# A fixed instruction order, a new order within a slot, more buffers and a two-step weight decode in a top-k attention kernel followed by a gated feed-forward layer

## The chip, the cores and the metric

The kernel runs on one core of a Trainium2 chip. The metric is the device time of one execution in microseconds; the median of the runs is reported. A profile is one execution recorded by the hardware profiler.

The core has five engines with a queue of instructions each: TensorE (PE, matrix products), VectorE (DVE), ScalarE (ACT), GpSimd (POOL) and SyncE (SP), which here only issues DMAs. They work side by side and meet at semaphores.

## The reference

Attention over 8 batches, 8 heads, 576 positions and 64 features keeps, for each query, the 32 largest scores. Its output, laid out as 4608 tokens of 512 features, goes through a layer of width 2048 with the gate h*cos(h).

```python
scores = scale * np.matmul(q, k.transpose(0, 1, 3, 2))
kth = np.partition(scores, -top_k, axis=-1)[..., -top_k:-top_k + 1]
scores = np.where(scores >= kth, scores, -1000000000.0)
attn = np.exp(scores - np.max(scores, axis=-1, keepdims=True))
attn = attn / (np.sum(attn, axis=-1, keepdims=True) + 1e-09)
attn_out = np.matmul(attn, v)
x = attn_out.transpose(0, 2, 1, 3).reshape(B * S, H * D)
h = x @ w_in
g = h * np.cos(h)
return g @ w_out
```

q, k and v are float32. The two weight matrices arrive as 64-bit floats, which the chip reads as pairs of 32-bit words, so the kernel turns them into float32 itself ("decode").

## The kernel before

**Units and slots.** The attention is cut into 144 units: 128 tokens times one pair of heads (four pairs a token tile). The main loop runs 146 slots. In slot i three units are at work: `u` = unit i is in its top-k search, `w` = unit i−1 in its softmax, `x` = unit i−2 is transposed and multiplied by v. The scores of unit i+2 are computed at the end of the slot.

**One unit.** `scores` (L184) writes 128x1152 scores to PSUM, one buffer, and ACT copies them to the tile `s` (L192). `topk_round` runs four times: two MAX8 (L206) find eight maxima each for the two heads, and two MATCH_REPLACE8 (L209, not in the fourth round) strike them out; all on DVE. `bounds` (POOL, L216 and L221) makes the mask's and the exponent's bias from the maxima. `softmax` runs two Prelu activations (L228), which push what is under the bound far down, and two exponentials with their sums (L233), on ACT. `add_eps` (POOL, L240), `reciprocal` (DVE, L246) and `normalise` (POOL, L251) finish it, the last in the next slot. `transpose_main` (L264, PE; copies to `pT`, L265, ACT), `transpose_tail` (L272, L273) and `values` (L289; copy to `xT`, L294) make the output. The tiles of the transposes and of the values share two PSUM buffers.

**The feed-forward layer in pieces.** Tokens form blocks: two of 128, sixteen of 256, two of 128. `ff1` makes one piece of the first product (L334): eight matmul instructions at 256 columns. Two pieces fill a PSUM tile, which ACT scales into half of a chunk `g` (L344); four pieces fill the chunk of 128x1024. A chunk is then reduced to a quarter-period argument `x` by four POOL instructions (L359 to L362), goes through the sine on ACT (`sines`, L372) and is multiplied back on POOL (`gates`, L379). There are 72 chunks. `ff2` makes a piece of the second product: two accumulation steps, four matmul instructions of 512 columns (L391); eight pieces make a token tile, scaled by ACT (L397) and stored by SP (L399). Both products have 288 pieces, 576 in all. After the last unit's search (`ff["end"]`) the reduction and the gate run on DVE instead (L350, L353, L379).

**The feeder.** `feed(n)` places up to n pieces on PE. Each slot adds 4.2 to a credit that is capped at 6, and a piece costs 1. It prefers `ff2` of the oldest block if the chunks it needs are gated and all weights are decoded. Otherwise it takes `ff1`, if the block's attention is complete, its weights are decoded and fewer than `CHUNKS` = 5 chunks are held; a block gives its chunks back only when its last `ff2` piece is placed. What is left after the 146 slots is placed by the last loop, two pieces an iteration.

**Weights.** There are 32 weight chunks of 512 KB. `load_weights` issues the DMA from SP into a buffer of tag `x`, of which there are `XB` = 3, shared with the sine arguments. `decode_weights` runs three ACT (L114, L115, L118), three DVE (L119, L120, L124) and two POOL instructions (L127, L128). Four chunks are decoded in each of the first slots.

**What sets the order.** The code runs inside a tile framework. Without further notice the framework reorders the instructions by its own planner: the order in which the functions are called gives a priority, and the planner decides when each instruction takes its place in its engine's queue. Once placed, the queue of an engine is worked off as placed.

Of the kernel before, what the change touches and what calls it, by code (L numbers as in the profile page):

```python
# [16 lines left out]
P = 128  # L17
# [13 lines left out]
def kernel(  # L31
# [7 lines left out]
    out: bass.AP,  # L39
):  # L40
    nc = tc.nc
    B, H, D, S = qT.shape
    DM, DF = moe_w_in.shape
    NT = S // P
# [43 lines left out]
        w_out.append(w)  # L88
        chunks.append((moe_w_out[f * P : (f + 1) * P, :], w))
    staged = {}  # L90
    CHUNKS, XB = 5, 3

    def load_weights(i):
        if i >= len(chunks):
            return
        src, dst = chunks[i]
        if not DECODE:
            nc.sync.dma_start(out=dst, in_=src)
            return
        st = ffw.tile([P, CW, 2], I32, tag="x", name="st", bufs=XB)  # L100
        nc.sync.dma_start(out=st.rearrange("p w i -> p (w i)"), in_=src)
        staged[i] = st

    def decode_weights(i):
        if not DECODE:
            return
        st = staged.pop(i)
        lo, hi = st[:, :, 0], st[:, :, 1]
        w = chunks[i][1]
        wi = w.bitcast(I32)  # L110

        both = ffw.tile([P, 2, CW], F32, tag="g", name="lo_sg", bufs=CHUNKS)
        r, sg = both[:, 0].bitcast(I32), both[:, 1]
        nc.scalar.mul(out=r, in_=lo.bitcast(U32), mul=2.0**-29)  # L114
        nc.scalar.sign(sg, hi)  # L115


        nc.scalar.activation(out=w, in_=hi.bitcast(F32), func=AF.Abs)  # L118
        nc.vector.tensor_scalar(out=w, in0=w, scalar1=2.0**-15, scalar2=None, op0=ALU.max)  # L119
        nc.vector.tensor_scalar(  # L120
            out=wi, in0=wi, scalar1=896 << 20, scalar2=3,
            op0=ALU.bitwise_xor, op1=ALU.logical_shift_left,
        )
        nc.vector.tensor_scalar(  # L124
            out=wi, in0=wi, scalar1=0x7FFFFFFF, scalar2=None, op0=ALU.bitwise_and
        )
        nc.gpsimd.tensor_tensor(out=wi, in0=wi, in1=r, op=ALU.add)  # L127
        nc.gpsimd.tensor_tensor(out=w, in0=w, in1=sg, op=ALU.mult)  # L128
# [46 lines left out]
            )  # L175

    def scores(u):
        sc = ps.tile([P, 2, 2, 512], F32, tag="sc", name="sc", bufs=1)
        for h in range(2):
            for j in range(2):  # L180
                d = slice(j * D, (j + 1) * D)
                for b, q0, rows, r0 in u["parts"]:
                    st = pairs[b, u["hp"]]
                    nc.tensor.matmul(  # L184
                        sc[r0 : r0 + rows, j, h, 0:HS],
                        st["q"][d, q0 : q0 + rows],
                        st["k"][d, h * HS : (h + 1) * HS],
                        start=True,
                        stop=True,
                    )  # L190
        s = u["s"] = work.tile([P, 2, S], F32, tag="s", name="s", bufs=5)
        nc.scalar.copy(  # L192
            out=s.rearrange("p j (h w) -> p (j h) w", h=2),
            in_=sc.rearrange("p j h w -> p (j h) w")[:, :, 0:HS],
        )

    def topk_round(u, rnd):
# [23 lines left out]
        nc.gpsimd.tensor_tensor(out=nd, in0=nb[:, :, 0], in1=nb[:, :, 1], op=ALU.subtract)  # L221
        u["nb"], u["nd"] = nb, nd

    def softmax(u):

        s, nb, nd = u["s"], u.pop("nb"), u.pop("nd")
        for j in range(2):
            nc.scalar.activation(  # L228
                out=s[:, j], in_=s[:, j], func=AF.Prelu, bias=nb[:, j, 1:2], scale=SCALE, alpha=FAR
            )  # L230
        den = u["den"] = small.tile([P, 2], F32, tag="den", name="den")
        for j in range(2):
            nc.scalar.activation(  # L233
                out=s[:, j], in_=s[:, j], func=AF.Exp, bias=nd[:, j : j + 1], scale=1.0,
                accum_out=den[:, j : j + 1],
            )
# [65 lines left out]
    for w in widths:  # L302
# [6 lines left out]
        t0 += w  # L309


    ff = {"live": 0, "now": 0, "weights": 0, "credit": 0.0, "end": False}
    first = deque((blk, i) for blk in blocks for i in range(2 * NF * blk["w"] // 512))
    second = deque(
        (blk, i, f) for blk in blocks for i in range(blk["w"] // P) for f in range(0, NF, 2)
    )
    waiting = deque()
    sined = deque()

    def ff1(blk, i):  # L320
        w = blk["w"]
        nf = 256 // w
        part = i % 4
        if part == 0:
            blk["g"].append(ffw.tile([P, 1024], F32, tag="g", name="g", bufs=CHUNKS))
            ff["live"] += 1
        if part % 2 == 0:
            blk["mm"] = ps.tile([P, 512], F32, tag="mm", name="mm")
        g, mm = blk["g"][-1], blk["mm"]
        for a in range(nf):  # L330
            f = i * nf + a
            at = (part % 2 * nf + a) * w
            for c in range(NC):
                nc.tensor.matmul(  # L334
                    mm[:, at : at + w],
                    w_in[f // FC][:, c, (f % FC) * P : (f % FC + 1) * P],
                    blk["xT"][:, c],
                    start=c == 0,
                    stop=c == NC - 1,
                )  # L340
        if part % 2 == 0:
            return
        half = part // 2
        nc.scalar.mul(out=g[:, half * 512 : half * 512 + 512], in_=mm, mul=INV_2PI)  # L344
        if half == 0:
            return
        x = ffw.tile([P, 1024], F32, tag="x", name="x", bufs=XB)
        if ff["end"]:

            nc.vector.tensor_scalar(  # L350
                out=x, in0=g, scalar1=0.25, scalar2=MAGIC, op0=ALU.add, op1=ALU.add
            )
            nc.vector.scalar_tensor_tensor(  # L353
                out=x, in0=x, scalar=MAGIC, in1=g, op0=ALU.subtract, op1=ALU.subtract
            )
            waiting.append((blk, g, x, ff["now"], -TWO_PI_BELOW))
            return
        gp = nc.gpsimd
        gp.tensor_scalar(out=x, in0=g, scalar1=1.0, scalar2=0.25, op0=ALU.mult, op1=ALU.add)  # L359
        gp.tensor_scalar(out=x, in0=x, scalar1=1.0, scalar2=MAGIC, op0=ALU.mult, op1=ALU.add)  # L360
        gp.tensor_scalar(out=x, in0=x, scalar1=-MAGIC, scalar2=1.0, op0=ALU.add, op1=ALU.mult)  # L361
        gp.tensor_tensor(out=x, in0=g, in1=x, op=ALU.subtract)  # L362
        waiting.append((blk, g, x, ff["now"], TWO_PI_BELOW))

    def sines(least):

        ready = [c for c in waiting if c[3] < ff["now"]]
        if not ready or (len(ready) < least and ready[0][3] + 4 > ff["now"]):
            return
        for blk, g, x, _, scale in ready:  # L370
            waiting.popleft()
            nc.scalar.activation(out=x, in_=x, func=AF.Sin, bias=halfpi, scale=scale)  # L372
            sined.append((blk, g, x))

    def gates():
        while sined:
            blk, g, x = sined.popleft()
            eng = nc.vector if ff["end"] else nc.gpsimd
            eng.tensor_tensor(out=g, in0=g, in1=x, op=ALU.mult)  # L379
            blk["gated"] += 1  # L380
# [40 lines left out]
            ff1(blk, i)  # L421
            n, ff["credit"] = n - 1, ff["credit"] - 1

    def decode(k):
        for _ in range(k):
            i = ff["weights"]
            if i < len(chunks):
                decode_weights(i)
                load_weights(i + 2)
                ff["weights"] += 1  # L430

# [11 lines left out]

    load_qk(0, 0)
    load_weights(0)
    load_qk(0, 1)
    load_weights(1)
    scores(units[0])  # L450
    for hp in range(2, NP):
        load_qk(0, hp)
    for hp in range(NP):
        load_v(0, hp)
    scores(units[1])
    for i in range(NU + 2):
        ff["end"] = i >= NU
        u = units[i] if i < NU else None
        w = units[i - 1] if 0 < i <= NU else None
        x = units[i - 2] if i > 1 else None  # L460
        for f, b, hp in at_slot.get(i, []):
            f(b, hp)
        ff["credit"] = min(ff["credit"] + 4.2, 6.0)
        ff["now"] += 1
        if w:
            bounds(w)
        if x:
            normalise(x)
        if u:
            topk_round(u, 0)  # L470
        decode(1)
        if w:
            softmax(w)
        gates()
        feed(2)
        if x:
            transpose_main(x)
        if u:
            topk_round(u, 1)
        decode(1)  # L480
        feed(1)
        if x:
            transpose_tail(x)
        feed(6)
        if w:
            add_eps(w)
        sines(2)
        if u:
            topk_round(u, 2)
        decode(1)  # L490
        if x:
            values(x)
        if i + 2 < NU:
            scores(units[i + 2])
        if u:
            topk_round(u, 3)
        if w:
            reciprocal(w)
        decode(1)
    while first or second:  # L500
        ff["now"] += 1
        ff["credit"] = 2.0
        gates()
        sines(1)
        feed(2)
        if ff["credit"] == 2.0:
            ff["now"] += 4


# [35 lines left out]
```

## Time and profile before

| | us |
|---|---|
| median of three runs (1831.09 to 1840.1) | 1837.81 |
| the profiled execution's own time | 1836.45 |
| its span, first to last instruction | 1834.7 |

Busy times by stage, in us:

| stretch of the span | PE | DVE | ACT | POOL | granted PE clock |
|---|---|---|---|---|---|
| 0 to 245.5 | 162.93 | 230.30 | 166.37 | 152.59 | 0.88 |
| 245.5 to 1645 | 1311.13 | 1238.33 | 969.83 | 698.14 | 0.98 |
| 1645 to 1834.7 | 167.66 | 34.76 | 37.31 | 3.45 | 0.98 |

In the first stretch the weights are decoded beside the first units, and few feed-forward pieces exist yet. In the second the units run one slot after the other with pieces between. In the third only feed-forward pieces are left, but for the last two units. The busy time of PE contains the filling of its pipeline at each start of a run of matmuls, so it overstates how much of it is used.

A timeline row gives the start, the duration, the engine, the line, the operation with its tiles, how often it follows itself (xcount), and in brackets how long the engine had been idle before and what released it. A row of the waits names who waited for whom, the total in us, how often, and the longest.

### The profile page before, as it was taken

What the parts mean: (1) busy time and instruction counts of PE and PEld (TensorE: products, weight loads), DVE (VectorE), ACT (ScalarE), POOL (GpSimd) and SP (SyncE); (2) the same over time, 40 slices, a digit from 0 to 9 for tenths busy, and PEclk for the clock granted to TensorE, in tenths of its full rate; (3) what the DMA queues carried; (4) which work ended last, traced back from release to release, by engine and by line L of the source; (5) the groups of instructions that cost most, each with busy time, mean ns of one, the idle gap of its engine ahead of it and who ended that gap; (6) DMA issues with size and microseconds to landing.
All of it is one profiled execution on the core that took longest, in us unless ns stands there. A gap on an engine that the chain in (4) does not pass through costs nothing.

```text
span 1834.7 us, 26443 instructions
## 1 busy us (share of the span) xinstructions
PE 1641.7 (89%) x9488; PEld 1077.8 (59%) x9488; DVE 1503.4 (82%) x3154; ACT 1173.5 (64%) x2056; POOL 854.2 (47%) x1103
## 2 busy tenths in 40 slices
PE   3477989989899989999999999999999999999897
PEld 2354566655656565565656575656666565656664
DVE  7999999979797878889797979899898979782211
ACT  5766768676667657576767676776767676762111
POOL 4786537362636535363636363554536363640000
PEclk9679989999999999999999999999999999999999
DMA  7430010001000110001000110011000100000000
GB/s 207 150 104 18 28 38 20 13 26 51 14 13 1 33 45 14 12 27 51 14 12 1 51 33 13 7 55 35 1 13 12 45 7 12 1 12 7 6 12 12
DMA packets 44228, 56.24 MB, mean 31 GB/s; under 512 B 10816, under 2 KB 27200, under 8 KB 44096
## 3 DMA queue, kind: packets, MB, share of 16 engines
q1 hardware_dynamic: 44096, 54.54, 9.6%
q8 instruction: 75, 1.23, 0.3%
q14 instruction: 57, 0.47, 0.1%
HBM read 45.09 MB, written 9.44 MB: 30 GB/s over the span
## 4 chain that ended last, share of the span: by engine, by line
DVE 52%; ACT 17%; POOL 15%; PE 12%; issue 3%; DMA 1%; SPq 0%; POOLq 0%; ACTq 0%
DVE m L206 27%; DVE rest L209 22%; PE o L391 6%; POOL x L362 5%; PE mm L334 4%; ACT s L228 4%; ACT s L233 3%; ACT x L372 3%; ACT s L192 2%; POOL x L359 2%; POOL x L361 2%; POOL x L360 2%; ACT L233 2%; ACT g L344 2%; PE o L289 1%
## 5 line engine op out<-in xcount | busy, mean ns | idle before, releaser
L206 DVE MAX8 m<-rest 128x8 f32<-128x576 f32 x864 | 611.1, 747 | 0.0
L334 PE MATMUL mm<-xT,w_in 128*128 128x256 f32 (+1 forms) x2560 | 551.3, 366 | 44.5 <-ACT g L344 40.3
L391 PE MATMUL o<-w_out,g 128*128 128x512 f32 x1152 | 539.7, 606 | 22.2 <-POOL g L379 11.5
L334 PEld LDWEIGHTS mm<-xT,w_in 128*128 128x128 f32 x2560 | 440.1, 193 | 142.8 <-ACT g L344 66.6
L209 DVE MATCH_REPLACE8 rest<-m,rest 128x576 f32<-128x576 f32 x576 | 423.4, 743 | 0.0
L391 PEld LDWEIGHTS o<-w_out,g 128*128 128x128 f32 x1152 | 207.8, 193 | 243.3 <-issue 217.3
L206 DVE MAX8 m<-s 128x8 f32<-128x576 f32 x288 | 203.4, 746 | 162.4 <-ACT s L192 162.4
L228 ACT ACTIVATE s<-s,nb 128x576 f32<-128x576 f32 x288 | 212.0, 773 | 145.4 <-POOL nb L216 145.4
L184 PE MATMUL sc<-k,q 64*128 64x288 f32 (+1 forms) x1280 | 239.6, 455 | 24.7 <-ACT s L192 15.3
L233 ACT ACTIVATE s<-s,nd 128x576 f32<-128x576 f32 x288 | 222.1, 772 | 2.1 <-POOL nd L221 1.3
L251 POOL TENSOR_SCALAR s<-s,rden 128x576 f32<-128x576 f32 x288 | 215.6, 749 | 1.3 <-DVE rden L246 0.7
L209 DVE MATCH_REPLACE8 rest<-m,s 128x576 f32<-128x576 f32 x288 | 211.7, 743 | 0.0
L216 POOL TENSOR_SCALAR nb<-m 128x4 f32<-128x4 f32 x144 | 29.6, 205 | 381.9 <-DVE rden L246 370.6
L264 PE MATMUL tp<-ident,s 128*128 128x128 f32 x1152 | 163.9, 282 | 40.0 <-POOL s L251 40.0
L264 PEld LDWEIGHTS tp<-ident,s 128*128 128x128 f32 x1152 | 136.2, 145 | 102.4 <-POOL s L251 54.8
L192 ACT COPY s<-sc 128x1152 f32<-128x1152 f32 x144 | 160.7, 1116 | 53.3 <-PE sc L184 52.2
L265 ACT COPY pT<-tp 128x512 f32<-128x512 f32 x288 | 154.3, 582 | 44.6 <-PE tp L264 44.6
L289 PEld LDWEIGHTS o<-pT,v 128*64 128x64 f32 x2560 | 134.9, 142 | 73.0 <-issue 36.9
L289 PE MATMUL o<-pT,v 128*64 128x128 f32 (+1 forms) x2560 | 171.7, 277 | 1.2 <-ACT pT L265 1.2
L184 PEld LDWEIGHTS sc<-k,q 64*128 64x128 f32 (+1 forms) x1280 | 115.1, 184 | 84.3 <-issue 37.3
L344 ACT ACTIVATE g<-mm 128x512 f32<-128x512 f32 x144 | 84.5, 587 | 125.2 <-PE mm L334 125.1
L379 POOL TENSOR_TENSOR g<-g,x 128x1024 f32<-128x1024 f32 x61 | 144.5, 2370 | 28.4 <-ACT x L372 25.1
(46 smaller groups left out, 1302.3 us busy)
## 6 DMA issues: line engine op xcount, KB each, us to landing
q<-in_q_dram SPq DMA_DIRECT2D x32, 288.0 KB, 3.0
out_dram<-ob SPq DMA_DIRECT2D x36, 256.0 KB, 2.0
st<-in_moe_w_in_dram SPq DMA_DIRECT2D x16, 512.0 KB, 5.2
v<-in_v_dram SPq DMA_DIRECT2D x32, 256.0 KB, 2.8
st<-in_moe_w_out_dram SPq DMA_DIRECT2D x16, 512.0 KB, 3.9
k<-in_k_dram SPq DMA_DIRECT2D x32, 144.0 KB, 3.3
k<-in_k_dram SPq DMA_DIRECT2D x32, 128.0 KB, 3.3
v_tail<-in_v_dram SPq DMA_DIRECT2D x64, 16.0 KB, 2.5
```

What stands on the lines that cost most here:

```text
L184: nc.tensor.matmul(sc[r0 : r0 + rows, j, h, 0:HS], st["q"][d, q0 : q0 + rows], st["k"][d, h * HS : (h + 1) * HS], start=True, stop=True,)
L192: nc.scalar.copy(out=s.rearrange("p j (h w) -> p (j h) w", h=2), in_=sc.rearrange("p j h w -> p (j h) w")[:, :, 0:HS],)
L206: nc.vector.max(m8[:, j, at], src[:, j])
L209: nc.vector.match_replace(rest[:, j], m8[:, j, at], src[:, j], NEG)
L228: nc.scalar.activation(out=s[:, j], in_=s[:, j], func=AF.Prelu, bias=nb[:, j, 1:2], scale=SCALE, alpha=FAR)
L233: nc.scalar.activation(out=s[:, j], in_=s[:, j], func=AF.Exp, bias=nd[:, j : j + 1], scale=1.0, accum_out=den[:, j : j + 1],)
L251: nc.gpsimd.tensor_scalar(out=s[:, j], in0=s[:, j], scalar1=rden[:, j : j + 1], scalar2=1.0, op0=ALU.mult, op1=ALU.mult,)
L264: nc.tensor.transpose(tp[:, c], s[:, j, k0 : k0 + P], ident)
L265: nc.scalar.copy(out=pT[:, :, j], in_=tp)
L289: nc.tensor.matmul(o[d, r], lhsT, rhs, start=c == 0, stop=c == NT)
L334: nc.tensor.matmul(mm[:, at : at + w], w_in[f // FC][:, c, (f % FC) * P : (f % FC + 1) * P], blk["xT"][:, c], start=c == 0, stop=c == NC - 1,)
L391: nc.tensor.matmul(o, g[:, at : at + P], w_out[f], start=f == 0, stop=f == NF - 1)
```

## The change

- `tc.manual_schedule()`: the instructions take their places in the engines' queues in the order in which the code issues them. The planner no longer moves any.
- `CHUNKS` goes from 5 to 8 and `XB` from 3 to 4.
- The weight decode is cut in two. `decode_first(i)` has the three ACT instructions, in a new order; `decode_second(i)` the DVE and POOL ones. One call of `decode()` issues the load of chunk i+2, the first half of chunk i and the second half of chunk i−1. There are three calls in a slot and one ahead of the loop, instead of four whole decodes in a slot.
- `scores` is split from `take_scores`, the copy to `s`. The copy of unit i+1 now stands in slot i behind the tail transpose. The first two units' scores, copies and loads are interleaved ahead of the loop.
- `softmax` is split into `mask`, at the head of the slot, and `exponentials`, behind the main transposes.
- `reciprocal` and `normalise` of unit i−1 both stand between rounds 2 and 3 of the slot. Before, the reciprocal stood behind round 3 and the normalisation in the next slot.
- The reduction is split: `reduce_first` (three POOL instructions) at the head of a slot and `reduce_second` (one) behind round 2, for the oldest chunk that is complete. At most one chunk is gated in a slot, by `gate(1)` at its head; before, all whose sines were out. `sines` takes all that wait, if there are two or the oldest is two slots old (before: four).
- `feed` is called with 1, 2 and 6 instead of 2, 1 and 6, and the last piece group stands ahead of `values`. The last loop gates, reduces, computes sines and gates again ahead of its two pieces.

```diff
+    ctx.enter_context(tc.manual_schedule())
...
-    CHUNKS, XB = 5, 3
+    CHUNKS, XB = 8, 4
...
+    def decode_first(i):
+        st = staged[i][0]
...
+        nc.scalar.activation(out=w, in_=hi.bitcast(F32), func=AF.Abs)
+        nc.scalar.sign(sg, hi)
         nc.scalar.mul(out=r, in_=lo.bitcast(U32), mul=2.0**-29)
+        staged[i] = [r, sg]
+
+    def decode_second(i):
+        r, sg = staged.pop(i)
...
+    def take_scores(u):
         s = u["s"] = work.tile([P, 2, S], F32, tag="s", name="s", bufs=5)
         nc.scalar.copy(
...
+    def reduce_second():
+        if not fresh or len(fresh[0]) < 3:
+            return
+        blk, g, x = fresh.popleft()
+        if not ff["end"]:
+            nc.gpsimd.tensor_tensor(out=x, in0=g, in1=x, op=ALU.subtract)
+        waiting.append((blk, g, x, ff["now"], -TWO_PI_BELOW if ff["end"] else TWO_PI_BELOW))
...
+        if not waiting or (len(waiting) < least and waiting[0][3] + 2 > ff["now"]):
+            return
...
+    def decode():
+        i = ff["step"]
+        if i > len(chunks):
+            return
+        ff["step"] += 1
+        load_weights(i + 2)
+        if i < len(chunks) and DECODE:
+            decode_first(i)
+        if i > 0:
+            if DECODE:
+                decode_second(i - 1)
+            ff["weights"] = i
```

The body of a slot after the change:

```python
        if w:
            bounds(w)
        gate(1)
        reduce_first()
        if u:
            topk_round(u, 0)
        decode()
        if w:
            mask(w)
        feed(1)
        if x:
            transpose_main(x)
        if w:
            exponentials(w)
        if u:
            topk_round(u, 1)
        decode()
        feed(2)
        if x:
            transpose_tail(x)
        if 0 < i < NU - 1:
            take_scores(units[i + 1])
        if w:
            add_eps(w)
        if u:
            topk_round(u, 2)
        decode()
        reduce_second()
        if w:
            reciprocal(w)
            normalise(w)
        feed(6)
        if x:
            values(x)
        sines(2)
        if i + 2 < NU:
            scores(units[i + 2])
        if u:
            topk_round(u, 3)
    while first or second:
        ff["now"] += 1
        ff["credit"] = 2.0
        gate(2)
        reduce_first()
        reduce_second()
        sines(1)
        gate(2)
        feed(2)
```

## The prediction

> **What bounds the kernel now.** I first read the page's engine totals and 40 slices.
>
> ```profile
> PE 1641.7 (89%) x9488; PEld 1077.8 (59%) x9488; DVE 1503.4 (82%) x3154; ACT 1173.5 (64%) x2056; POOL 854.2 (47%) x1103
> ...
> PE   3477989989899989999999999999999999999897
> ...
> DVE  7999999979797878889797979899898979782211
> ```
>
> DVE is full for about 245 us, both engines are nearly full until 1645 us, and then PE works almost alone. So there are three stages: 245, 1400 and 190 us. The waits and the Vector timeline show how full the middle really is.
>
> ```profile
> DVE m L206 <- ACT s L192: 162.4, 53, 10.0
> ...
> 602.00 0.14 DVE L246 RECIPROCAL rden<-den 128x2 f32<-128x2 f32 x1
> ...
> 611.70 0.15 DVE L246 RECIPROCAL rden<-den 128x2 f32<-128x2 f32 x1
> ...
> 662.38 1.42 DVE L206 MAX8 m<-s 128x8 f32<-128x576 f32 x2 [2.73 <-ACT s L192]
> ```
>
> From reciprocal to reciprocal an unhindered slot takes DVE 9.70 us (column one is the start). A wait for the score copy is added in a third of the slots. The first bounds of slot 17 run at 245.52 and the last maximum ends at 1644.94, so 127 slots took 1399 us: **11.02 us each**, 1.32 above what DVE needs. What does PE need? Its busy time contains pipeline fills, so I take distances from start to start.
>
> ```profile
> 1627.64 1.09 PE L289 MATMUL o<-pT,v 128*64 128x128 f32 x16
> 1628.57 0.39 PE L289 MATMUL o<-pT_tail,v_tail 128*64 128x128 f32 x4
> 1628.88 1.24 PE L184 MATMUL sc<-k,q 64*128 64x288 f32 x8
> 1630.06 3.70 PE L391 MATMUL o<-w_out,g 128*128 128x512 f32 x8
> 1633.59 1.04 PE L264 MATMUL tp<-ident,s 128*128 128x128 f32 x8
> 1634.47 1.88 PE L391 MATMUL o<-w_out,g 128*128 128x512 f32 x4
> ...
> 1636.18 0.27 PE L272 MATMUL tp<-ident,s 128*128 128x128 f32 x1
> 1636.29 1.88 PE L391 MATMUL o<-w_out,g 128*128 128x512 f32 x4
> ...
> 1663.25 3.71 PE L334 MATMUL mm<-xT,w_in 128*128 128x256 f32 x16
> 1666.80 1.02 PE L391 MATMUL o<-w_out,g 128*128 128x512 f32 x2
> ...
> 1821.33 9.27 PE L391 MATMUL o<-w_out,g 128*128 128x512 f32 x16 [5.18 <-DVE g L379]
> ```
>
> Attention costs PE 1628.88−1627.64 for values, 1.18 for scores, 0.88 and 0.11 for transposes: 3.41 us a slot. A piece of `ff2` (four matmuls) takes 3.53/2 = 1.77, one of `ff1` (eight at 256 columns) 3.55/2 = 1.77; the 46 matmuls from 1678.58 to 1698.42 give 1.73. I use 1.75. A slot with four pieces needs 3.41+7.00 = 10.4 us of PE. So neither engine explains 11.02: the middle is bound by waits between them.
>
> **How many pieces the loop places.** I followed the feeder's counters (4.2 credit a slot, cap 6, block complete, chunk gated, free chunks) through all 146 slots. Old rules: 32 pieces before slot 17, 464 in the 129 slots 17 to 145, 80 left of 576. The trace agrees: L350, the tail's form, ran 11 times, and 34 `ff1` pieces left plus 8 of slots 144 and 145 make 10.5 chunks. New rules: 32, 503 and **41 left**. With 5 chunk buffers the new rules still leave only 43, with 8 the old leave 41; either edit alone nearly suffices.
>
> **The change, part by part.**
> *First stage.* Decode keeps its three ACT, three DVE and two POOL instructions per chunk. The DVE six groups sum to 14.0+13.0+12.0+11.5+11.2+10.3 = 72 us; 17 slots x 9.70 + 72 + 10.9 of start is 248 against 245 in the trace. Three steps a slot instead of four shift the last decode from slot 7 to 10 and the first `ff2` from slot 9 to 10, while PE is nearly idle: nothing. The score copy no longer stands behind L114 (9.20 to 9.86): at best −1.5. One L119 to L124 ran 0.40 to 1.50 us, so 96 of them lie between 38 and 144: −34 to +72, and I take the row's sum, since the same POOL work stands beside them. On SP the weight load is issued two steps ahead, over 10 us, against 5.2 to land; behind it stand q, k, v loads needed slots later and output stores. Nothing, or 5 us of one late load in a stage without slack.
> *Middle stage.* Written order on one slot, times from PE's start: one piece to 1.75, main transposes to 2.6, two pieces to 6.1, tail 6.2, one piece 8.0, values 9.2, scores 10.4. ACT: mask (1.45), eviction 0.6, two pT copies to about 3.5, table load if due (1.28), exponentials 1.6, second eviction, tail copy 0.27 at 6.9, score copy to 8.4. So DVE may start its next unit at 8.4, 2.0 us before PE's next slot; the reciprocal, moved ahead of round 3, is due 8.3 into DVE's slot, at 6.3, and exponentials plus eps are done at 5.4, with a load 6.7. Slots of four pieces run at PE's 10.4. In a slot of six the extra pieces lie behind the score copy, so DVE leads by up to 5.5 us and light slots use that lead. A nine-slot cycle from the count, with pieces 5,3,0,2,6,4,4,4,4: PE sum 86.7, DVE sum 87.3; carried through slot by slot with those two limits, and with transposes no earlier than 1.3 after DVE's slot start (normalise ends there), it takes 94.9, or 10.55.
> *Sines.* Now in pairs at a slot's end: 1.28+1.15+1.05 = 3.5 behind the xT copy at 9.6 reaches 2.7 into the next slot. Mask, copies and exponentials queue behind it, values on PE slip by 1.3. Of the two pairs in a cycle one falls into a light slot and is hidden: 1.3/9 = 0.15 a slot. So **10.7 x 129 = 1380 us**. From below, perfect averaging is PE's sum, 129x3.41+503x1.75 = 1320. From above, no averaging at all (23 slots of three or fewer pieces at 9.7, 75 at 10.4, 15 at 12.2, 16 at 13.9) is 1408, and a 3.5 us stall for each of 34 sine groups 1527. I take 1380, as the rows for DVE and PE are regular and the lead is real.
> *The fourth sine buffer.* POOL's first reduction step, L359, waited 96.4 us in all, every bit for ACT's eviction of g and none for a free buffer: nothing, and nothing to lose.
> *New waits.* POOL's gate waits for a sine; behind it stand reduce, eps, second reduce, normalise, and for these the DVE reciprocal and PE's transposes. A slot with gate and reduction fills POOL with 0.4+2.37+3.15+0.2+2.37+1.5 = 10.0 us; the count has 28 such slots, 39 with a reduction alone. At zero in the forecast: covered by the 2.0 us lead.
> *Table loads.* Sines and exponentials switch 62 and 61 times now:
>
> ```profile
> L372 ACT ACT_TABLE_LOAD x62 | 79.5, 1283 | 1.1
> ...
> L233 ACT ACT_TABLE_LOAD x61 | 78.3, 1283 | 1.1
> ```
>
> The count has 34 sine groups in the loop, 55 loads fewer: 70 us of ACT, off the path, worth only the slack above. The load at 610.70 is followed by its sine at 611.99, so nothing hides beside the 1.28. The Trainium skill, "ScalarE: Activation LUTs", section "What ACT_TABLE_LOAD costs", gives about 2.66 us a switch with a drain, an estimate of 146 us for the 55; this trace shows no such drain.
> *Idle PE.* After the 3.50 us wait at 679.16 eight `ff1` matmuls took 3.27 instead of 1.89, so an idle array runs slower. The 14 new slots of at most one piece each risk 1.4: 20 us if exposed, and hidden since DVE sets those slots. The Trainium skill's "TensorE: Matmul & The Clock Gate", Part 1, says an idle window of some 3.4 us halves the clock; that speaks against lumpy slots, and by it the sum would be some 20 us higher as an estimate, if DVE did not set them.
> *Tail.* 41 x 1.75 = 72. The new end loop gates a chunk in the iteration after its last `ff1`, with no `ff1` between: the chain eviction, two DVE steps, sine, gate is bare, 5.18 in the row at 1821.33. The count has four such places, 21, plus 4 for the first. The last 16 matmuls took 9.27 instead of 7.0, and eviction and store follow to 1834.7: 6.4. Together **103**, against 190.
>
> **Sum:** 245+1380+103 = 1728 of span; the profiled run's time is 1.75 above its span (1836.45 against 1834.7) and the median 1.4 above that run: **1731 us**.
>
> **Rivals.**
> *A, only the tail shrinks (faster).* The fixed order loses as many waits as it cures and slots stay at 11.02: 245+129x11.02+103+3 = **1773**. For it: four dependent engines with nothing to reorder round a late one. Against it: the 162 us of score waits come from copies placed late, and the new place is fixed.
> *B, POOL's fixed queue becomes the clock (slower).* Gate waits for a sine done 2.8 into PE's slot, the reduction follows, eps comes behind both, so reciprocal, round 3 and the next mask slip. It decides from (1837−1731)/67 = 1.6 us in each of the 67 reduction slots. At 2.2 each: 1731+147 = **1878**. For it: 10.0 us of POOL in a 9.7 us slot, two new in-order waits. Against it: POOL is 47% busy, and the next slots are light.
> *C, no net gain.* Pieces moved into the loop lengthen it by what the tail loses; the middle goes to 11.6: **1837**. Against it: PE has 1.5 us unused in each slot today. That the change doesn't do what it says would also end here: if the placement of pieces were as before, 80 would be left. The rules exclude it.
>
> **How the numbers follow.** Forecast 0.52, A 0.22, B 0.20, C 0.06. Predicted is the forecast's 1731; its own range is 1690 (half way to perfect averaging, and a quieter tail) to 1790 (each sine group exposed by half). Up to 1845 takes in A, C and B's mild end; below 1690 and above 1845 I leave some 2 in 10. Half a percent, 9 us, is what a measurement here tells from no change (the three runs spread over 9): forecast and A are faster, 0.74; C gives 0.05 same and 0.01 faster; slower 0.20.
>
> **What would show it.** Right: median slot near 10.7 between the bounds of slot 17 and the last maximum; L206's wait for the score copy far below 162; six chunks on DVE in the tail (L350's form x6, POOL's x66); about 38 table loads each way; tail near 103 us with four gaps of 5 us. Wrong: DVE idle ahead of the reciprocal (eps or exponentials late), which is B; PE idle ahead of transposes waiting for normalise; a first stage beyond 265.

## The result, and the profile after

The changed kernel takes **1988.99 us** (median of four runs, 1985.88 to 1993.21) against 1838.95 (four runs, 1831.09 to 1840.19) for the kernel before: ratio 1.083, 95% interval 1.079 to 1.087. It is 150 us slower; 1731 was forecast. The profiled run took 1993.21, its span is 1991.4.

First the page of the changed kernel, its engine totals and the 40 slices:

```profile
PE 1666.5 (84%) x9488; PEld 1099.2 (55%) x9488; DVE 1481.4 (74%) x3139; ACT 1109.3 (56%) x2002; POOL 894.9 (45%) x1128
...
PE   3659887979798877989898989898988889898887
...
DVE  7999886778787876768687777868696969695511
...
PEclk9968897989899898999999999999898989898999
```

DVE's slices fall to 6, 7 and 8 from the second stage on, and alternate between 6 and 9 in the last third. PE has as many instructions as before and 25 us more busy time, and its clock drops to 8 again and again. The waits of the changed kernel:

```profile
POOL den L249 <- ACT s L242: 677.9, 134, 11.5
DVE rden L255 <- POOL den L249: 334.9, 79, 12.3
ACT pT L274 <- PE tp L273: 279.0, 104, 5.8
...
PE o L413 <- POOL g L401: 142.3, 42, 6.0
POOL g L401 <- ACT x L394: 132.7, 28, 8.3
...
DVE m L212 <- ACT s L198: 66.7, 61, 8.0
```

The wait for the score copy fell from 162 us to 67, as forecast. In its place DVE stands 335 us ahead of the reciprocal (12.9 before). The lines hang together: the reciprocal (second line) waits for eps on POOL, eps (first line) for the exponentials on ACT, ACT's copies of the transposes (third line), which stand ahead of the exponentials, for PE. And PE waits 142 us, 42 times, for a gated chunk.

The stages, from one table each of busy time by stretch, cut at the bounds of slot 17 and at the end of PE's last attention product (columns: stretch; its length; busy time of PE, PEld, DVE, ACT, POOL with instruction counts; granted PE clock; DMA):

```profile
0.00:236.70 236.70, 149.65 (x894) 102.21 (x895) 216.53 (x453) 155.57 (x287) 151.45 (x178) 0.88 0.33 98
236.70:1886.40 1649.70, 1436.67 (x8276) 949.75 (x8274) 1249.91 (x2672) 938.82 (x1697) 743.45 (x951) 0.94 0.06 19
1886.40:1991.40 105.00, 80.21 (x322) 47.29 (x320) 14.94 (x14) 14.89 (x19) 0.00 (x0) 0.93 0.03 11
```

Forecast were 245, 1380 and 103; measured are 237, **1650** and 105. The whole miss lies in the middle: 129 slots at 12.79 us instead of 10.7.

From slot 73 on an eight-slot cycle repeats, by the distances of the bounds: 13.5, 8.3, **24.3**, 13.7, 11.3, 9.7, 9.7, 11.9, together 102.4 us. The feeder's counters give these slots 1, 6, 4, 4, 4, 4, 5 and 4 pieces, and a gate in the third to the sixth. The long slot begins at 1282.50. Its rows from the timeline of PE, ACT, POOL and DVE, with others between them left out:

```profile
1288.31 1.24 PE L188 MATMUL sc<-k,q 64*128 64x288 f32 x8
1288.43 0.27 ACT L303 COPY xT<-o 128x128 f32<-128x128 f32 x1 [0.65 <-PE o L298]
1288.71 1.28 ACT L394 ACT_TABLE_LOAD   x1
...
1290.01 2.19 ACT L394 ACTIVATE x<-x,halfpi 128x1024 f32<-128x1024 f32 x2
...
1291.23 2.35 POOL L401 TENSOR_TENSOR g<-g,x 128x1024 f32<-128x1024 f32 x1 [8.26 <-ACT x L394]
...
1293.64 3.78 PE L413 MATMUL o<-w_out,g 128*128 128x512 f32 x4 [4.08 <-POOL g L401]
...
1297.22 1.91 PE L273 MATMUL tp<-ident,s 128*128 128x128 f32 x8
...
1298.31 0.59 ACT L274 COPY pT<-tp 128x512 f32<-128x512 f32 x1 [4.79 <-PE tp L273]
...
1299.77 1.28 ACT L242 ACT_TABLE_LOAD   x1
...
1301.06 0.78 ACT L242 ACTIVATE s<-s,nd 128x576 f32<-128x576 f32 x1
...
1302.77 0.19 POOL L249 TENSOR_SCALAR den<-den 128x2 f32<-128x2 f32 x1 [5.92 <-ACT s L242]
...
1303.00 0.17 DVE L255 RECIPROCAL rden<-den 128x2 f32<-128x2 f32 x1 [12.22 <-POOL den L249]
```

PE is through with the scores at 1289.6. The next instruction in its queue is a piece of the second product, and it reads the chunk that POOL gates in this same slot; the gate waits for the first of a pair of sines, and these stand behind the xT copy at the slot's end and behind a table load. So PE stands still for 4.08 us. Then its four matmuls take 3.78 instead of 1.88 and eight transposes 1.91 instead of 1.04; the granted clock there is 0.50. The copies, the exponentials queued behind them on ACT, eps and the reciprocal follow: DVE has waited 12.22 us.

### The profile page after: what moved, and what is told of

The parts are those of the page before. It is cut to its first block, busy times and chain, and to the rows that moved or that the text cites. A ratio compares the mean times of both kernels' runs of the same rounds, so it can differ in the third digit from the quotient of the medians.

```text
span 1991.4 us, 26254 instructions
## 1 busy us (share of the span) xinstructions
PE 1666.5 (84%) x9488; PEld 1099.2 (55%) x9488; DVE 1481.4 (74%) x3139; ACT 1109.3 (56%) x2002; POOL 894.9 (45%) x1128
## 4 chain that ended last, share of the span: by engine, by line
PE 63%; ACT 12%; DVE 11%; POOL 9%; issue 4%; DMA 1%; SPq 0%; POOLq 0%; ACTq 0%
PE o L413 27%; PE mm L344 20%; PE o L298 6%; PE tp L273 5%; POOL g L401 5%; PE sc L188 4%; DVE m L212 4%; DVE rest L215 4%; ACT s L242 3%; POOL s L260 3%; ACT g L354 2%; ACT pT L274 2%; ACT x L394 1%; ACT L394 1%; ACT L242 1%
## 5 line engine op out<-in xcount | busy, mean ns | idle before, releaser
L413 PE MATMUL o<-w_out,g 128*128 128x512 f32 x1152 | 608.2, 668 | 161.2 <-POOL g L401 142.3
L344 PEld LDWEIGHTS mm<-xT,w_in 128*128 128x128 f32 x2560 | 434.3, 191 | 152.7 <-ACT g L354 68.4
L413 PEld LDWEIGHTS o<-w_out,g 128*128 128x128 f32 x1152 | 223.7, 210 | 409.3 <-issue 226.3
L249 POOL TENSOR_SCALAR den<-den 128x2 f32<-128x2 f32 x144 | 28.4, 197 | 678.8 <-ACT s L242 677.9
L255 DVE RECIPROCAL rden<-den 128x2 f32<-128x2 f32 x144 | 23.3, 162 | 335.1 <-POOL den L249 334.9
L188 PE MATMUL sc<-k,q 64*128 64x288 f32 (+1 forms) x1280 | 193.3, 449 | 43.7 <-ACT s L198 31.8
L273 PEld LDWEIGHTS tp<-ident,s 128*128 128x128 f32 x1152 | 156.9, 159 | 107.2 <-issue 66.4
L401 POOL TENSOR_TENSOR g<-g,x 128x1024 f32<-128x1024 f32 x66 | 155.9, 2363 | 132.7 <-ACT x L394 132.7
L273 PE MATMUL tp<-ident,s 128*128 128x128 f32 x1152 | 174.1, 301 | 29.2 <-POOL s L260 29.0
L298 PE MATMUL o<-pT,v 128*64 128x128 f32 (+1 forms) x2560 | 166.2, 274 | 2.4 <-ACT pT L274 2.4
```

Of the source, the lines that this page charges most:

```text
L188: nc.tensor.matmul(sc[r0 : r0 + rows, j, h, 0:HS], st["q"][d, q0 : q0 + rows], st["k"][d, h * HS : (h + 1) * HS], start=True, stop=True,)
L273: nc.tensor.transpose(tp[:, c], s[:, j, k0 : k0 + P], ident)
L298: nc.tensor.matmul(o[d, r], lhsT, rhs, start=c == 0, stop=c == NT)
L344: nc.tensor.matmul(mm[:, at : at + w], w_in[f // FC][:, c, (f % FC) * P : (f % FC + 1) * P], blk["xT"][:, c], start=c == 0, stop=c == NC - 1,)
L413: nc.tensor.matmul(o, g[:, at : at + P], w_out[f], start=f == 0, stop=f == NF - 1)
```

## Experiments

Theory 1: PE's first piece of a slot waits in order for the gate of its own slot, and the rest of the slot is late with it. Rivals: POOL's queue (B of the prediction), the place of the exponentials, the new order of calls as such. Each run below is one profile and one time unless a number of runs is given; the kernel before, on the same chip beside them, took 1839.79, 1837.46 and 1836.47 (median of nine) in the three sets.

**A gated chunk counts from the next slot on.** Only the counter moves, so PE takes a piece whose input is ready.

```diff
-            blk["gated"] += 1
+            if ff["end"]:
+                blk["gated"] += 1
+            else:
+                fresh_gated.append(blk)
...
         ff["now"] += 1
+        while fresh_gated:
+            fresh_gated.pop()["gated"] += 1
```

> The changed kernel, but ff2 may use a chunk only from the slot after the one that gates it (slots 0 to 143). Theory 1 (PE stands at the head of the slot before an ff2 whose chunk POOL is gating in the same slot; transposes, ACT copies, exponentials and DVE's reciprocal wait behind it): PE's wait for POOL g falls from 142 us to under 30, DVE's wait before the reciprocal from 335 to under 150, time 1760 to 1850. Theory 2 (the exponentials' place behind the pT copies on ACT is the cause, whatever holds PE): the reciprocal wait stays above 250, time above 1920.

1840.38 us: 149 us less by the counter alone. PE's wait for POOL is gone from the list, the reciprocal's wait is more than halved. But the slots still take 11.69 us. Waits of this kernel:

```profile
DVE rden L255 <- POOL den L249: 149.7, 72, 6.2
...
DVE m L212 <- ACT s L198: 104.3, 67, 7.8
...
PE mm L345 <- ACT g L355: 78.5, 57, 3.9
```

**The exponentials right behind the mask**, so that they don't queue behind the copies of the transposes; once on the changed kernel, once with the counter edit:

```diff
             mask(w)
+            exponentials(w)
         feed(1)
...
-        if w:
-            exponentials(w)
```

> The changed kernel with the exponentials straight behind the mask, ahead of the slot's first piece and the main transposes. Theory 1: DVE's wait before the reciprocal falls, but PE's wait for POOL g stays at 120 to 160 us and PE sets the time: 1890 to 1960. Theory 2: the coupling is gone and with it the loss: below 1850.

> Both edits together. Theory 1: little more than the late gate alone, 1740 to 1840. Theory 2: as the early exponentials alone, within 1%.

1898.41 and 1857.73. On the changed kernel the move saves 91 us: the exponentials no longer inherit PE's lateness. PE's wait for the gate stays as well, though at 101 us, under the 120 to 160 expected. Where PE is not late (with the counter edit) it costs 17 us: DVE's wait for the score copy goes from 104 to 198 us and PE's wait ahead of the tail transpose from 15 to 60, probably because ACT now takes the exponentials ahead of what PE needs. The second expectation was missed; the place of the exponentials passes the delay on and is not its source.

**The planner back**, with all other parts of the change kept:

```diff
-    ctx.enter_context(tc.manual_schedule())
```

> The changed kernel without the line that fixes the order, so the planner places the new code. If the fixed queue is what turns a late gate into a standstill (theory 1), the planner defers the ff2 and the time is near the kernel before or better, 1750 to 1860, with PE's wait for POOL g under 60. If the new order of calls is bad by itself, 1900 or more.

1888.64, between the two expectations. PE's wait for the gate is absent here too, so the planner did not leave that piece standing at the head of PE's queue. DVE's wait for the score copy is 211.8. So fixing the order costs this version 100 us, and the new order of calls with its buffers costs about 50 even under the planner.

**A second wait behind the first.** With the counter edit PE waits 78 us for ACT to evict a first-product tile (48 in the changed kernel, 40 in the kernel before). Rows of that kernel, PE's and ACT's:

```profile
1290.17 1.89 PE L345 MATMUL mm<-xT,w_in 128*128 128x256 f32 x8
1295.93 2.68 PE L345 MATMUL mm<-xT,w_in 128*128 128x256 f32 x8 [3.87 <-ACT g L355]
```

```profile
1292.48 1.28 ACT L242 ACT_TABLE_LOAD   x1
...
1295.31 0.57 ACT L355 ACTIVATE g<-mm 128x512 f32<-128x512 f32 x1
```

The piece in the second row needs the PSUM tile that the piece in the first row filled, and its eviction stands behind table load and exponentials on ACT. Yet the tag `mm` has two buffers. In the instruction order the other is held by a half-done second product: 12 of its 16 steps were placed, the chunk for the last four was not gated yet, and the feeder turned to the next block's first product. Theory 3: let a token tile's second product begin only when all chunks of its block are gated.

```diff
-                if blk["gated"] * 1024 // blk["w"] >= f + 2 and ff["weights"] == len(chunks):
+                if blk["gated"] * 1024 // blk["w"] >= NF and ff["weights"] == len(chunks):
```

It ran with the counter edit, alone on the changed kernel, and alone on the kernel before:

> The late gate, and ff2 of a token tile starts only when all chunks of its block are gated. Theory 3: what is left after the late gate (slots of 11.7 us instead of 10.7) comes from an ff2 accumulator that stands half done in one of the two PSUM buffers of tag mm while the next block's ff1 runs, so that ff1 has one buffer and waits for ACT's eviction, which stands behind the exponentials. Then PE's wait for ACT g falls from 78 us to under 20 and the time from 1840 to 1730 to 1790. Rival (ACT's or POOL's queue alone sets the slots): PE's wait for g may fall, but the time stays within 1820 to 1850.

> The changed kernel with the whole-block rule alone: the chunk gated last still lets ff2 start in the same slot, so the bare gate wait comes once for a block instead of up to four times. Theories 1 and 3 together: PE's wait for POOL g 142 to between 40 and 80 us, PE's wait for ACT g under 25, time 1780 to 1880. If the late gate alone mattered, 1900 or more.

> The kernel before with the whole-block rule: the same open accumulator there (PE waits 40 us for ACT g, 0.69 us at each pair of ff1 pieces in the tail). Theory 3: 10 to 50 us faster, PE's wait for ACT g under 15. Against it: with 5 chunk buffers a block of four chunks that gives none back until it is complete leaves the next block one chunk, so the rule may starve ff1: 0 to 40 us slower.

Together with the counter edit **1712.48**, alone 1727.58, on the kernel before 1829.68. The first is better than expected. Waits of that kernel:

```profile
POOL den L249 <- ACT s L242: 499.6, 117, 9.0
...
DVE rden L255 <- POOL den L249: 103.3, 77, 6.2
...
DVE m L212 <- ACT s L198: 45.4, 37, 7.9
```

PE has no wait left for POOL's gate, and 0.4 us for the eviction of its first product. Its middle and its tail, in the columns used above, behind the middle of the kernel with the counter edit alone:

```profile
230.97:1736.76 1505.79, 1393.54 (x8277) 931.84 (x8269) 1247.49 (x2670) 936.74 (x1699) 750.68 (x956) 0.98 0.07 21
...
231.00:1627.60 1396.60, 1357.63 (x8251) 924.12 (x8251) 1244.61 (x2670) 929.31 (x1698) 753.35 (x957) 0.99 0.07 23
1627.60:1710.70 83.10, 78.57 (x336) 47.26 (x336) 13.80 (x13) 13.62 (x18) 0.00 (x0) 0.99 0.04 13
```

Nearly the same matmuls as in the changed kernel's middle (8251 and 8276) cost 79 us less busy time at a clock of 0.99 instead of 0.94, and PE's idle time there falls from 1649.70−1436.67 = 213 us to 39. These two make the 253 us of the middle. Another 22 come from the tail, where PE's five waits for DVE's gates are gone, and 6 from the first stage. Of the 128 us that the rule adds to the counter edit, 109 lie in the middle: PE's idle time there falls from 112 us to 39, about what the wait for the eviction was, and its busy time by 36.

The rule alone was expected to leave a wait of 40 to 80 us for the gate and missed on the fast side. When the fourth chunk of a block is gated, the product now starts at the block's first chunk, gated slots earlier. So one rule removes both waits, and the counter edit adds only 15 us to it. On the kernel before, the wait for the eviction goes from 40 to 0, but the wait of the tail transposes for ACT's copies goes from 50 to 73: 8 us in one run, where that kernel's own runs span 9, so it is unclear.

**The buffers alone on the kernel before:**

```diff
-    CHUNKS, XB = 5, 3
+    CHUNKS, XB = 8, 4
```

> The kernel before with 8 chunk and 4 sine buffers and nothing else: the feeder's count leaves 41 pieces for the tail instead of 80. If placing pieces earlier were worth their PE time as the forecast assumed, the tail falls by 39 x 1.75 = 68 us and the time to 1760 to 1800; if the loop's slots grow by what the tail loses (rival C), 1820 to 1850.

1855.1, a little over the expected band. The tail shrinks, and the slots grow from 11.02 to 11.74, which over 127 slots is 91 us: what rival C of the prediction describes, with DVE's wait for the score copy up to 222.

**The last set** took the version with both rules: timed, under the planner, with 7 chunk buffers, and with the gate moved on POOL's queue.

```diff
-    ctx.enter_context(tc.manual_schedule())
...
-    CHUNKS, XB = 8, 4
+    CHUNKS, XB = 7, 4
```

```diff
-        gate(1)
         reduce_first()
...
             normalise(w)
+        gate(1)
         feed(6)
```

> The kernel with both cures (a gated chunk usable from the next slot on, and the second product of a token tile only when all chunks of its block are gated), timed in rounds beside the kernel before. Its one earlier run took 1712.5 us against 1837.5. Theory 1 (the middle's extra time of the changed kernel is PE's in-order wait for a gate of its own slot, and the PSUM buffer that a half-done product holds): the gain is real and repeats, 1705 to 1725 us, ratio to the kernel before 0.925 to 0.94. Rival (the one run was lucky): over 1740.

> The same kernel, with the instructions placed by the planner again; only the line of the fixed order goes. With no late producer at the head of PE's queue left, the two ways of placing differ by what the fixed order itself is worth. Theory 1 (the fixed order does no harm of its own; it pays once its waits are gone, because the score copy and the exponentials stand where they are written): 1740 to 1850 us, with DVE's wait for the score copy back above 120 us. Rival (the planner does all that the fixed order does, and mends what is late besides): 1680 to 1720.

> The same kernel with 7 chunk buffers instead of 8. By the feeder's counters 46 pieces are left for the tail instead of 45, but slots of 2 and 6 pieces alternate more often. Theory 1 (buffers matter by the pieces they leave and by the unevenness of slots): 1705 to 1745. Rival (the eighth buffer is what keeps the middle going): over 1760.

> The same kernel with the gate of a slot moved on POOL's queue from ahead of the reduction to behind the normalisation; the chunk is usable from the next slot on, as in the kernel it is made from. It tells whether POOL's fixed queue costs time of its own (rival B of the prediction: the gate waits for a sine, and the reduction, eps and the reciprocal slip with it). Rival B: DVE's wait ahead of the reciprocal falls from 103 us to under 60, and the time to 1650 to 1690. Theory 1 (eps waits for the exponentials on ACT, not for POOL): that wait stays at 80 to 120 us and the time at 1695 to 1735.

*Timed:* 1712.13 (five runs, 1711.55 to 1713.56) against 1836.47 (nine runs): ratio **0.933, 0.931 to 0.935**. It beats both kernels.

*Under the planner:* 1888.58, slower than either expectation. The planner gives the same time with the two rules as without them (1888.64):

| order of calls | planner | fixed |
|---|---|---|
| before | 1837 | not tried |
| after | 1889 | 1989 |
| after, both rules | 1889 | 1712 |

The planner's version waits elsewhere, for the copies of scores that the fixed order puts in their place:

```profile
DVE m L212 <- ACT s L198: 247.6, 90, 5.4
```

So the fixed order costs 100 us with the gate's piece at the head of PE's queue and gains 176 with both rules.

*Seven buffers:* 1779.99, which misses 1705 to 1745; the rival's "over 1760" came. The counters leave 46 pieces for the tail instead of 45, so the loss is not there: the slots go from 10.84 to 11.38 us, 69 us over 127 slots. The pieces come as 2, 6, 4, 2, 6, 4, 4, 4 instead of 1, 6, 4, 4, 4, 4, 5, 4, the same 32, and the cycle takes 91.4 us instead of 86.7, on average of six. Waits of this kernel:

```profile
DVE rden L255 <- POOL den L249: 177.7, 64, 6.1
ACT pT L274 <- PE tp L273: 169.9, 94, 3.3
...
POOL g L402 <- ACT x L395: 125.5, 31, 6.1
```

The eighth buffer is worth 68 us here. That the second pair of a light and a full slot is the reason fits the lengths (slots of 14.0 and 14.7 us follow the two slots of six pieces; with eight buffers the longest are 13.1 to 14.0 and 13.4), but was not shown by itself. Taking each slot at the longer of DVE's 9.70 and PE's sum, the second pair adds 1.0 us to the cycle, of the 4.7 measured. More of the loss shows as slower matmuls: in the middle PE is busy 1394.80 us here at a granted clock of 0.96, against 1357.63 at 0.99.

*The gate behind the normalisation:* 1732.0. Rival B expected DVE's wait ahead of the reciprocal under 60 and 1650 to 1690; the wait rose to 122.3 and the time by 20. Theory 1's band of 80 to 120 was missed by 2 us, its time was met. POOL's fixed queue, with the gate in front, is not what makes the reciprocal late in this version; on the changed kernel itself the gate was not moved.

## Why the prediction was wrong

**First stage:** 245 forecast, 237 measured, in part by luck. The six groups of the decode on DVE took 53.5 us, not 72, and DVE's first maximum started 2.0 us earlier; so some 12 us, an estimate, were lost again elsewhere. Single instructions of the decode had run up to 2.51 us before, not 1.50. One weight load came late, as the prediction allowed: ACT stood 8.52 us for it until 28.80, and the stage still ended early.

**Counts:** right in all. The groups of the changed kernel:

```profile
L401 POOL TENSOR_TENSOR g<-g,x 128x1024 f32<-128x1024 f32 x66 | 155.9, 2363 | 132.7 <-ACT x L394 132.7
...
L394 ACT ACT_TABLE_LOAD x35 | 44.9, 1283 | 0.6
...
L242 ACT ACT_TABLE_LOAD x34 | 43.6, 1283 | 0.6
...
L401 DVE TENSOR_TENSOR g<-g,x 128x1024 f32<-128x1024 f32 x6 | 7.3, 1224 | 13.6 <-ACT x L394 13.6
```

Sixty-six chunks are gated on POOL and six on DVE; there are 35 and 34 table loads, against some 38 forecast; and of the 322 matmuls in the tail's stretch 320 are the 41 pieces counted (28 of four, and 13 of sixteen at 128 columns).

But the cycle carried through for the middle was not the one that repeats. By the same counters the nine slots of 5, 3, 0, 2, 6, 4, 4, 4 and 4 pieces come twice, in slots 29 to 46; from slot 65 on it is eight slots of 1, 6, 4, 4, 4, 4, 5 and 4. PE needs 10.41 us a slot in these, against 9.63 in the nine, so 10.55 a slot for the whole stage left too little.

**Tail:** 103 forecast, 105 measured. The bare gates are five waits:

```profile
1890.50 8.57 PE L413 MATMUL o<-w_out,g 128*128 128x512 f32 x16 [4.08 <-DVE g L401]
...
1920.66 8.83 PE L413 MATMUL o<-w_out,g 128*128 128x512 f32 x16 [3.33 <-DVE g L401]
...
1940.91 8.83 PE L413 MATMUL o<-w_out,g 128*128 128x512 f32 x16 [2.38 <-DVE g L401]
...
1960.21 7.13 PE L413 MATMUL o<-w_out,g 128*128 128x512 f32 x16 [3.33 <-DVE g L401]
...
1978.77 8.81 PE L413 MATMUL o<-w_out,g 128*128 128x512 f32 x16 [5.11 <-DVE g L401]
```

They sum to 18.2 us, against 25 taken, while PE is busy 80 us for pieces forecast at 72 and slowed last matmuls at 2. So the sum is close in part by luck.

**Score wait and lead:** the wait for the score copy fell to 67 as named. That light slots use DVE's lead is hardly seen, even in the version with both rules. Its cycle takes 86.4 to 88.0 us, where PE needs 8x3.41 + 32x1.75 = 83.3 and DVE 8x9.70 = 77.6; with no lead at all, each slot at the longer of the two, it would be 87.8. Its whole middle takes 1397 us, 10.83 a slot, against 1412 so worked out from its own counts. So with both waits gone the lead is worth some 15 us net of other delays, an estimate, where the forecast counted 28 (1408 to 1380).

**The step that failed** is "New waits", priced "At zero in the forecast: covered by the 2.0 us lead". It asked what stands behind the gate on POOL, and not who waits for the gated chunk. That is PE: by the counters a piece of the second product is first in PE's queue in each slot with a gate, and in two of the four such slots of a cycle it reads the chunk that is gated there. The timeline of a slot, "one piece to 1.75", let that piece run without asking for its input. The paragraph on the sines puts them at a slot's end, "behind the xT copy at 9.6", so the lateness could be read from it: sines until 2.7 into the next slot and 2.37 for the gate set that piece free at about 5 instead of 0. By the rows it was 4.08 us late, and the cover of 2.0 us was too small for it even without the slower clock behind it. Sized from the runs: the counter edit takes away 149 us, the rule on the product 261 (with it the second wait, for the PSUM tile, goes too), both 277. The forecast missed by 258.

Of the rivals, B had the right sign and a time 111 us short, and the sign "DVE idle ahead of the reciprocal" that it named. Its first step came true too: the gate waits for a late sine, 132.7 us in all. But its mechanism, reduction and eps late on POOL's queue, is not the one: of POOL's 678.8 us of idle time ahead of eps 677.9 ended with the exponentials, and in the version with both rules moving the gate out of eps's way made nothing faster. A and C were 216 and 152 us too low (C's own 11.6 a slot sums to 1847, not 1837); what C describes is what the larger buffers do to the kernel before. Of the other two signs that were to show it wrong, neither came: PE waits 29 us for the normalisation (40 before), and the first stage is short. "Idle PE" was priced at 20 us and hidden "since DVE sets those slots"; in the long slot it added 1.90 us to the matmuls and 0.87 to the transposes, on top of the 4.08 of waiting.

Left open: the order of calls of the kernel before under a fixed order wasn't tried, nor the new order of calls with the old number of buffers, and the halves of the decode, the sines in pairs and the fourth sine buffer were not run by themselves.

## What to carry to other kernels

Before the order of an in-order queue is fixed, write beside each instruction at the head of a stage where its input comes from in that same stage: an instruction that reads what another engine makes in the same slot holds up everything behind it. Here a counter that hands the product on one slot later took the wait away, worth 149 us. An accumulation that is begun before all its inputs exist keeps its PSUM buffer, and the work that fills the pause then runs with one buffer fewer. A fixed order and such edits have to be tried together: here the edits were worth nothing under the planner (1889 with and without) and 277 us under the fixed order.

## What the runs showed of the hardware

Short waits of PE make the matmuls behind them slower, but not always. Stretches of the changed kernel, the first in its long slot and three in its tail (columns: stretch; its length; busy time of PE with instruction count; granted PE clock; DMA):

```profile
1293.60:1299.20 5.60, 5.56 (x13) 0.50 0.00 0
1920.75:1924.15 3.40, 3.40 (x4) 0.50 0.00 0
1941.25:1944.60 3.35, 3.35 (x5) 0.50 0.02 5
1960.21:1967.30 7.09, 7.08 (x18) 1.00 0.00 0
```

In the long slot a wait of 4.08 us was followed by four matmuls in 3.78 us instead of 1.88. In the tail two waits had the same length, 3.33 us: sixteen matmuls took 8.83 us after the one, at half the clock for the first 3.4 us of them, and 7.13 after the other, at full clock. After a wait of only 2.38 us they took 8.83. So the length of a wait alone does not tell what follows it. The Trainium skill, "TensorE: Matmul & The Clock Gate", Part 1, says that the clock halves after an idle window of some 3.4 us and that the window is free-running. The tail's rows agree with the second half, since equal waits had unequal ends; the 2.38 us are under the length that the page names, so a wait need not be that long.

Over a whole stage it shows as busy time: 1436.67 us for 8276 matmuls at a granted clock of 0.94, 1357.63 for 8251 at 0.99. A busy PE is then no sign that PE does more.
